# Exclusive decay sums made by VectorE from the inclusive ones, with one PSUM bank instead of two for the sums

## The chip, the cores and the metric

The kernel runs on one core of a Trainium2 chip. The metric is the device time of one execution in microseconds. Every kernel was timed in several rounds beside the kernel before on the same chip. A run counts as slow when it is more than 1.5% above the fastest run of the same kernel.

## The reference

Two layers in a row. A recurrent attention with a decay per channel (4 batches, 8 heads, 768 steps, head dimension 40), and then a layer that mixes all 768 steps of a batch with two 768 x 768 matrices:

```python
def _attn_ref(r, k, v, w, a, b):
    for t in range(S):
        y[:, :, t] = einsum('bhd,bhde->bhe', r_t, state)
        Sa = einsum('bhde,bhe->bhd', state, a_t)
        state = state * w_t[..., None] - einsum('bhd,bhe->bhde', Sa, b_t) \
                + einsum('bhd,bhe->bhde', v_t, k_t)

def _moe_ref(x, w_theta, w_tok_r, w_tok_i, w_ch):
    theta = x @ w_theta
    yr = einsum('ts,bsd->btd', w_tok_r, x * cos(theta))
    yi = einsum('ts,bsd->btd', w_tok_i, x * sin(theta))
    u = x + yr + yi
    return u + maximum(u @ w_ch, 0)
```

The kernel works in chunks of 128 steps, 24 of them ("tiles" below). Within a chunk it needs the products of the decays `w` up to each step: inclusive (with the step's own) for `k` and `b`, exclusive (without it) for `a` and the output. It makes them as exponentials of sums of logarithms.

## The kernel before

TensorE makes both running sums, with two triangular matrices, into the two banks of a pair. ScalarE takes the exponential of both, and of the chunk's total decay, in one instruction:

```python
def cs():
    t = ps(pk)                                   # a pair of PSUM banks
    nc.tensor.matmul(t[:, 0, 512 - DM:512], lhsT=ntri_inc, rhs=lw[:, :, 0:D], ...)
    nc.tensor.matmul(t[:, 1, 0:DM], lhsT=tri_exc, rhs=lw[:, :, 0:D], ...)
    nc.tensor.matmul(t[:, 1, DM:DM + 8], lhsT=ident, rhs=off_diag, ...)
    for g in range(G):                           # the chunk's total decay
        nc.tensor.matmul(t[:, 1, DM + 2 * g:DM + 2 * g + 2], lhsT=pair(lw, g), rhs=ones2, ...)
add("PE", "cs", i, cs, 2 * mm(320) + 5 * 25, [("lw", s2)], [pk], new=(pk, 2), ...)
add("ACT", "exp", i, lambda: nc.scalar.activation(
    out=ex, in_=ps(pk).rearrange("p a b -> p (a b)")[:, 512 - DM:512 + DM + 8],
    func=AF.Exp), 710, [pk], [kex], table="lnexp")
```

No operation is issued as it is written. `add` records it with its engine, its assumed duration and what it reads and writes; then all of them, some 1,500, are put into one order, by priorities that a search has tuned (the tables `OFF`, `TIMES` and `ADJ`), and issued in it. Each engine works through its own part of that order, one instruction after the other: in the eight traces of the changed order (the changed kernel and seven experiments) ScalarE's 390 instructions come in one and the same sequence. What the plan takes for a dependency:

```python
pre = set(after)
for r in reads:                       # a reader waits for the writer
    if r in self.writer:
        pre.add(self.writer[r])
for w in writes:                      # a writer waits for the writer and the readers before
    if w in self.writer:
        pre.add(self.writer[w])
    pre.update(self.readers.get(w, ()))
```

## Time and profile before

| | before |
|---|---|
| time, median of 3 runs | 214.62 us (214.03 to 215.32) |
| span of the profiled run, granted clock | 211.9 us, 0.996 |
| TensorE busy from 20 to 72 us | 48.32 of 52 us |
| TensorE busy from 72 to 205 us | 132.93 of 133 us |

The lines themselves stand in the prediction. The simplest reading comes from the last two rows: what TensorE does not use of the 185 us between 20 and 205 us is 3.68 + 0.07 = 3.75 us. "Busy" includes a matmul's latency (0.30 us for one whose successor starts 0.13 us later, in the prediction's timeline), so it says nothing of how well TensorE is used; but where it is *not* busy, it had nothing to do. I call that figure TensorE's idle time.

How the two engines that make the decays wait is told by the list of waits (the waiting engine and line, what ended the wait; us in total, times, longest). Before, the only direction is TensorE to ScalarE, and GpSimd, which multiplies `k` and `b` by the decays:

```profile
POOL kb L686 <- ACT ex L678: 18.4, 4, 12.1
...
ACT ex L678 <- PE ps_d L674: 3.9, 7, 0.9
```

And this is one tile's decays in the timeline (start us, us): one instruction, between two others.

```profile
89.20 0.44 ACT L898 COPY th<-ps_s 128x320 f32<-128x320 f32 x1
89.52 0.73 ACT L678 ACTIVATE ex<-ps_d 128x648 f32<-128x648 f32 x1
90.12 0.31 ACT L827 COPY gd<-ps_s 128x160 f32<-128x160 f32 x1
```

### The profile page before, as it was taken

What the parts mean: (1) busy time and instruction counts of PE and PEld (TensorE: products, weight loads), DVE (VectorE), ACT (ScalarE), POOL (GpSimd) and SP (SyncE); (2) the same over time, 40 slices, a digit from 0 to 9 for tenths busy, and PEclk for the clock granted to TensorE, in tenths of its full rate; (3) what the DMA queues carried; (4) which work ended last, traced back from release to release, by engine and by line L of the source; (5) the groups of instructions that cost most, each with busy time, mean ns of one, the idle gap of its engine ahead of it and who ended that gap; (6) DMA issues with size and microseconds to landing.
All of it is one profiled execution on the core that took longest, in us unless ns stands there. A gap on an engine that the chain in (4) does not pass through costs nothing.

```text
span 211.9 us, 8102 instructions
## 1 busy us (share of the span) xinstructions
PE 198.8 (94%) x3365; PEld 155.7 (74%) x3365; DVE 166.2 (78%) x253; ACT 152.1 (72%) x342; POOL 117.4 (55%) x173
## 2 busy tenths in 40 slices
PE   7767999989999999999999999999999999999993
PEld 3445788767777788788787877788778787877761
DVE  7477787897879799789898677887889898946443
ACT  4475867999799868977949789777898757573011
POOL 3203365798877674885981859773658440751000
PEclk9999999999999999999999999999999999999998
DMA  6998999999999999995989889989896100002122
GB/s 116 193 169 167 171 212 161 164 172 182 189 170 195 177 193 199 179 164 69 247 163 201 162 150 216 153 191 170 184 193 123 34 3 33 3 3 94 67 91 93
DMA packets 134181, 30.82 MB, mean 145 GB/s; under 512 B 125824, under 2 KB 134144, under 8 KB 134144
## 3 DMA queue, kind: packets, MB, share of 16 engines
q1 hardware_dynamic: 131712, 27.54, 66.5%
q0 software_dynamic: 2432, 2.77, 9.0%
q8 instruction: 26, 0.43, 0.9%
q14 instruction: 11, 0.09, 0.1%
HBM read 29.13 MB, written 3.93 MB: 156 GB/s over the span
## 4 chain that ended last, share of the span: by engine, by line
PE 68%; DVE 6%; ACT 4%; issue 2%; DVEq 0%; ACTq 0%
PE ps_s L942 19%; PE ps_s L616 11%; PE ps_d L740 9%; PE ps_s L888 8%; PE ps_s L843 4%; DVE phi L745 2%; PE ps_s L809 2%; PE ps_s L723 2%; PE ps_s L791 2%; PE ps_s L872 2%; PE ps_s L990 1%; PE ps_s L870 1%; PE ps_s L863 1%; PE ps_d L666 1%; PE ps_s L779 1%
## 5 line engine op out<-in xcount | busy, mean ns | idle before, releaser
L686 POOL TENSOR_TENSOR kb<-raw_kb,ex 128x320 bf16<-128x320 f32 x44 | 37.2, 861 | 18.4 <-ACT ex L678 18.4
L942 PE MATMUL ps_s<-zr,wtok_r 128*128 128x320 bf16 x144 | 41.0, 300 | 0.0
L942 PE MATMUL ps_s<-zi,wtok_i 128*128 128x320 bf16 x144 | 40.8, 299 | 0.0
L690 POOL TENSOR_TENSOR ah<-raw_a,ex 128x320 bf16<-128x320 f32 x22 | 19.0, 864 | 30.6 <-issue 17.0
L745 DVE TENSOR_TENSOR lamu<-ps_d,mask_p 128x1024 bf16<-128x1024 f32 x24 | 29.3, 1220 | 7.0 <-PE ps_d L740 6.6
L745 DVE TENSOR_TENSOR phi<-ps_d,mask_n 128x1024 bf16<-128x1024 f32 x24 | 29.3, 1219 | 4.5 <-PE ps_d L740 4.2
L745 DVE TENSOR_TENSOR lamv<-ps_d,mask_p 128x1024 bf16<-128x1024 f32 x24 | 29.2, 1219 | 3.9 <-PE ps_d L740 3.7
L745 DVE TENSOR_TENSOR psi<-ps_d,mask_p 128x1024 bf16<-128x1024 f32 x24 | 29.2, 1216 | 1.5 <-PE ps_d L740 1.5
L924 POOL TENSOR_TENSOR zi<-cs,x 128x320 bf16<-128x320 f32 x23 | 17.7, 789 | 10.3 <-ACT cs L912 10.1
L924 POOL TENSOR_TENSOR zr<-cs,x 128x320 bf16<-128x320 f32 x23 | 17.7, 789 | 6.8 <-ACT cs L912 6.8
L678 ACT ACTIVATE ex<-ps_d 128x648 f32<-128x648 f32 x24 | 17.1, 713 | 5.1 <-PE ps_d L674 3.9
L619 ACT COPY uT<-ps_s 128x192 f32<-128x192 f32 x24 | 7.5, 319 | 15.5 <-PE ps_s L843 14.2
L879 DVE TENSOR_TENSOR x<-ps_s,ex 128x320 bf16<-128x320 f32 x24 | 11.7, 487 | 7.8 <-PE ps_s L872 3.7
L740 PE MATMUL ps_d<-aT,kbT 64*128 64x128 bf16 x384 | 16.6, 218 | 0.9 <-ACT kbT L619 0.7
L942 PEld LDWEIGHTS <-wtok_r 128*128 128x128 bf16 x144 | 14.0, 97 | 4.5
L942 PEld LDWEIGHTS <-wtok_i 128*128 128x128 bf16 x144 | 14.1, 98 | 3.5
L619 ACT COPY kbT<-ps_s 128x512 f32<-128x512 f32 x24 | 14.2, 590 | 3.3 <-PE ps_s L616 3.2
L952 DVE TENSOR_TENSOR u<-ps_s,x 128x320 bf16<-128x320 f32 x24 | 11.7, 489 | 6.0 <-PE ps_s L942 5.3
L961 DVE SCALAR_TENSOR_TENSOR oo<-ps_s,u 128x320 f32<-128x320 f32 x24 | 11.6, 488 | 5.2 <-PE ps_s L888 4.3
L870 PE MATMUL ps_s<-kb,lamv 128*128 128x40 bf16 x192 | 15.4, 180 | 0.0
L872 PE MATMUL ps_s<-kb,lamu 128*128 128x40 bf16 x192 | 15.0, 180 | 0.1
L616 PE MATMUL ps_s<-ident,kb 128*128 128x128 bf16 x192 | 14.7, 219 | 0.1
(117 smaller groups left out, 562.3 us busy)
## 6 DMA issues: line engine op xcount, KB each, us to landing
raw_v<-in_v_dram SPq DMA_DIRECT2D x24, 160.0 KB, 3.8
raw_w<-in_w_dram SPq DMA_DIRECT2D x24, 160.0 KB, 4.5
raw_kb<-in_k_dram SPq DMA_DIRECT2D x24, 160.0 KB, 4.3
raw_a<-in_a_dram SPq DMA_DIRECT2D x24, 160.0 KB, 3.9
raw_kb<-in_b_dram SPq DMA_DIRECT2D x24, 160.0 KB, 3.9
raw_r<-in_r_dram SPq DMA_DIRECT2D x24, 160.0 KB, 3.4
out_dram<-oo SPq DMA_DIRECT2D x24, 160.0 KB, 1.9
wrow_i<-in_moe_w_tok_i_dram POOLq DMA_DIRECT2D x6, 192.0 KB, 5.0
```

The source lines that it names most:

```text
L616: nc.tensor.transpose(out=dst[:, c:c + 128], in_=pair(src, g), identity=ident)
L619: nc.scalar.copy(out=out.bitcast(FP32), in_=in_)
L678: add("ACT", "exp", i, lambda: nc.scalar.activation(out=ex, in_=ps(pk).rearrange("p a b -> p (a b)")[:, 512 - DM:512 + DM + 8], func=AF.Ex ...
L686: lambda j=j: (nc.vector if fast else nc.gpsimd).tensor_tensor(out=paired(kb[:, j])[:, :, :, 0:D], in0=natural(raw_kb[s4][:, j]), in1=invW ...
L690: lambda: (nc.vector if fast else nc.gpsimd).tensor_tensor(out=paired(ah)[:, :, :, 0:D], in0=natural(raw_a[i % 6]), in1=Wi, op=ALU.mult),
L740: nc.tensor.matmul(t[:, q, g, :], lhsT=lhs[rows(q), g * 128:(g + 1) * 128], rhs=rhs[rows(q), g * 128:(g + 1) * 128], start=True, stop=True)
L745: add("DVE", kindm, i, lambda: nc.vector.tensor_tensor(out=dst.rearrange("p a b c -> p (a b) c"), in0=ps(p).rearrange("p a (g c) -> p (a g ...
L870: nc.tensor.matmul(o, lhsT=lamv[:, p, g, :], rhs=kb[:, 0, h, 0:D], start=first, stop=False, skip_group_check=True)
L872: nc.tensor.matmul(o, lhsT=lamu[:, p, g, :], rhs=kb[:, 1, h, 0:D], start=False, stop=True, skip_group_check=True)
L888: nc.tensor.matmul(dst, lhsT=lhs[:, kt, :], rhs=rhs[:, kt, :], start=kt == 0, stop=kt == 2)
L924: nc.vector if fast else nc.gpsimd).tensor_tensor(
L942: nc.tensor.matmul(ps(pk)[:, 0:DM], lhsT=wtok[nm][:, s, j * 128:(j + 1) * 128], rhs=zs[c][:, s], start=n == 0 and c == 0, stop=n == NT - 1 ...
```

## The change

The intent: an exclusive sum is the inclusive sum less the step's own term. So one of the two 320-column matmuls can go, VectorE makes the exclusive sums by an add, and the sums fit into one bank, which leaves both pairs of banks to the score products. The price is an add on VectorE, and three exponentials in place of one.

```diff
         def cs():
             t = ps(pk)
-            nc.tensor.matmul(t[:, 0, 512 - DM:512], lhsT=ntri_inc, rhs=lw[:, :, 0:D], ...)
-            nc.tensor.matmul(t[:, 1, 0:DM], lhsT=tri_exc, rhs=lw[:, :, 0:D], ...)
+            nc.tensor.matmul(t[:, 0:DM], lhsT=ntri_inc, rhs=lw[:, :, 0:D], ...)
 ...                                       (the total decay: now into columns 320 to 327, sign turned)
-        add("PE", "cs", i, cs, 2 * mm(320) + 5 * 25, [("lw", s2)], [pk], new=(pk, 2),
+        add("PE", "cs", i, cs, mm(320) + 5 * 25, [("lw", s2)], [pk], new=(pk, 1),
             tail=tail(2))
         add("ACT", "exp", i, lambda: nc.scalar.activation(
-            out=ex, in_=ps(pk).rearrange("p a b -> p (a b)")[:, 512 - DM:512 + DM + 8],
-            func=AF.Exp), 710, [pk], [kex], table="lnexp")
+            out=ex[:, 0:DM], in_=ps(pk)[:, 0:DM], func=AF.Exp), 432, [pk], [kex], table="lnexp")
+        sx = rw_t[i % 2]
+        add("DVE", "wi", i, lambda: nc.vector.tensor_tensor(
+            out=sx[:, 0:DM].rearrange("p (h d) -> p h d", h=H),
+            in0=ps(pk)[:, 0:DM].rearrange("p (h d) -> p h d", h=H), in1=lw[:, :, 0:D], op=ALU.add),
+            490, [pk, ("lw", s2)], [("rw", i % 2)])
+        add("ACT", "ew", i, lambda: nc.scalar.activation(
+            out=ex[:, DM:2 * DM], in_=sx, func=AF.Exp, scale=-1.0),
+            432, [("rw", i % 2)], [kw], table="lnexp")
+        add("ACT", "ewm", i, lambda: nc.scalar.activation(
+            out=ex[:, 2 * DM:2 * DM + 8], in_=ps(pk)[:, DM:DM + 8], func=AF.Exp, scale=-1.0),
+            180, [pk], [kwm], table="lnexp")
 ...                                       (users of ex wait for the part that they read)
-OFF = dict(...)  TIMES = dict(...)  ADJ = {...}
+OFF = dict(...)  TIMES = dict(...)  ADJ = {...}      (all priorities searched anew)
```

## The prediction

> **What bounds the kernel now.** I read the page's engine row first, then its slices, then the sums by stretch, the chain of waits, and last the groups that the change touches.
>
> ```profile
> PE 198.8 (94%) x3365; PEld 155.7 (74%) x3365; DVE 166.2 (78%) x253; ACT 152.1 (72%) x342; POOL 117.4 (55%) x173
> ...
> PE   7767999989999999999999999999999999999993
> ...
> DMA  6998999999999999995989889989896100002122
> ...
> PE 68%; DVE 6%; ACT 4%; issue 2%; DVEq 0%; ACTq 0%
> ```
>
> TensorE looks like the bound, but 94% is an average over two regimes. The DMA digits are full up to about 160 us and then fall away. The sums by stretch separate the regimes (columns: length, busy time and instructions of each engine, clock, DMA share, GB/s):
>
> ```profile
> 20.00:72.00 52.00, 48.32 (x961) 39.55 (x962) 44.83 (x50) 44.68 (x103) 38.00 (x54) 1.00 1.01 180
> 72.00:205.00 133.00, 132.93 (x2199) 104.98 (x2198) 105.89 (x143) 95.46 (x215) 75.10 (x104) 1.00 0.68 132
> ```
>
> Up to 72 us the DMA share is 1.01: the inputs of a tile (six transfers of 160 KB, 0.98 MB) at 180 GB/s take 5.5 us, an estimate from that row, and the starts of the decay sums show ten tiles between 5 and 58 us, 5.3 us each. So the transfers pace this part, with VectorE (44.83 of 52, 86%) and ScalarE (44.68, 86%) not far behind. From 72 us on the token mixing of earlier batches is a stock of ready TensorE work: TensorE is busy for 132.93 of 133.00 us, and the chain of waits is nearly all matmuls there. What is taken from TensorE after 72 us comes off the end; what is taken before is mostly hidden under the transfers.
>
> "Busy" counts a matmul's whole latency, so a matmul's price must be read from starts. The timeline of one tile's decay sums, in a saturated stretch:
>
> ```profile
> 114.54 0.30 PE L666 MATMUL ps_d<-lw,ntri_inc 128*128 128x320 bf16 x1
> 114.67 0.30 PE L668 MATMUL ps_d<-lw,mask_p 128*128 128x320 bf16 x1
> 114.81 0.17 PE L670 MATMUL ps_d<-off_diag,ident 128*128 128x8 bf16 x1
> 114.84 0.24 PE L674 MATMUL ps_d<-ones,lw 128*128 128x2 bf16 x4
> ```
>
> Each 320-column matmul reads 0.30 us, but the next starts 0.13 to 0.14 us later. That is its price. The other groups concerned (busy time, mean ns, idle before, releaser):
>
> ```profile
> L678 ACT ACTIVATE ex<-ps_d 128x648 f32<-128x648 f32 x24 | 17.1, 713 | 5.1 <-PE ps_d L674 3.9 <-POOL r L715 0.8 <-issue 0.2
> ...
> L659 ACT ACTIVATE lw<-raw_w 128x320 bf16<-128x320 f32 x24 | 11.5, 478 | 3.0 <-DMA raw_w<-in_w_dram 3.0
> ...
> L898 ACT COPY th<-ps_s 128x320 f32<-128x320 f32 x23 | 9.9, 429 | 4.2 <-PE ps_s L888 3.9
> L817 DVE TENSOR_TENSOR gt<-ps_s,ex 128x320 bf16<-128x320 f32 x20 | 9.7, 487 | 2.9 <-PE ps_s L809 2.4 <-ACT nuT L619 0.2
> ```
>
> **What the Trainium skill says.** "TensorE: Matmul & The Clock Gate", section "Back-to-back issue gap", gives N/2.4 + 2.5 ns for a warm matmul: 136 ns for 320 columns. The trace agrees (0.13 to 0.14 us). "VectorE: DVE Perf Modes", section "The TRN2 errata", gives an fp32 two-tensor add (N + 151)/0.96 = 491 ns; the trace's 128x320 operations with a PSUM input take 487. "ScalarE: Activation LUTs", section "What ACT_TABLE_LOAD costs", gives 186 + 0.833 N ns with immediate scale and bias, so a scale of -1 costs nothing extra, and about 93 ns of overlap between neighbours. For 648 columns that is 726 against 713 measured; in the timeline one ScalarE copy of 0.58 us starts at 40.34 and the next exponential at 40.82, so the overlap is 0.10. "PSUM — Partial Sum Buffer", section "PSUM bank collisions raise a hardware error", says two engines must not read one bank at once. Before, ScalarE alone reads the sums; now VectorE reads the same bank too, so the two reads have to be ordered. No run here shows that yet.
>
> **The change, part by part.**
>
> Removed: one 320-column matmul per tile and its weight load. 24 x 136 ns = 3.26 us of TensorE issue. The trace has 11 of these before 72 us and 13 after. The 13 are worth 13 x 0.136 = 1.77 us of the end. The 11 (1.50 us) fall where TensorE waits for data and earn nothing directly. The small matmuls of the chunk decay stay: one of 8 columns and four of 2, with the sign turned.
>
> Added on VectorE: one 128x320 add per tile, 487 ns in the trace for such a form. Neighbours overlap by 0.08 us (gt starts 63.41 and the next 63.81, 0.40 apart), so 0.40 us of engine time each, 24 x 0.40 = 9.6 us; busy time grows by 24 x 0.487 = 11.7 us to about 178.
>
> Changed on ScalarE: one exponential of 648 columns (713 ns) becomes three: 320 from PSUM (429, like the copy of th), 320 from SBUF (between 429 and the 478 of lw; I take 465) and 8 columns (about 165, from the straight line through copies of 160 columns at 292 and 512 at 590 ns). 429 + 465 + 165 - 713 = +346 ns of busy time a tile, +8.3 us in all, but with two more overlaps of 0.10 only about 0.15 us of engine time a tile, 3.5 us.
>
> Moved in time: the inverse decays that k and b wait for come about 0.136 + 0.28 = 0.42 us earlier. The decays for a go through matmul, (ordered) exponential, add, exponential: 0.43 + 0.49 + 0.465 against 0.71, so some 0.7 us later if the reads are ordered, less 0.136. Four buffers of ex and the run-ahead of a tile's preparation should hide this, except for the first tile.
>
> Banks: the sums leave the two pairs of banks, which only the score products use now, for the pool of four single banks. Scores in 64-row mode come in 65 runs in the issue order I read from the trace: 34 of one product (426 ns median until other work starts) and 31 of two (648). Joining two single runs saves 2 x 426 - 648 = 204 ns. After 72 us there are 11 single runs; with free pairs I expect two or three joins, -0.5 us. Against it, a single bank is held longer (matmul, exponential, add, small exponential, some 2 us); I charge +0.3 us for waits of other work.
>
> Where added work can reach the end: from 60 to 71 us VectorE runs without a gap (busy 11.97 of 12 from 60 to 72), while the stock of mixing work is not there yet. Two adds in that stretch are 0.8 us; I charge half, +0.4.
>
> The order: all priorities were searched anew for the new costs. That cannot be costed from a row; an order made for a lighter TensorE and a heavier VectorE should recover some of the early idle time. I allow -0.7.
>
> Sum: -1.77 - 0.5 + 0.3 + 0.4 - 0.7 = -2.3 us; 214.6 - 2.3 = 212.3.
>
> **Rivals.** First, VectorE becomes a joint bound. For it: 86% up to 72 us, saturated from 60 to 72, and 9.6 us more engine time; early tiles take 5.2 us and VectorE would use about 4.9 of it. Against: 105.89 of 133 us after 72 leaves 27 us for 13 x 0.40 = 5.2, and the transfers pace the early part. If it wins, mixing starts 1 to 3 us later and the time is 214 to 216. Second, the freed bank pairs matter more than the matmul: VectorE's waits for score products (16.1 us of idle before the four masked products) shrink, the early part tightens and all 3.26 us count, with more joins. For it: those waits are VectorE's largest. Against: early, the transfers are full whatever the banks do, and late the waits are on a busy TensorE, not on banks. It would give 209 to 211. Third, transfers set the last tile: their share stays near 1 to about 160 us, so nothing that TensorE saves ends sooner. Against: between 72 and 205 us TensorE never idles, and the mixing that fills it needs no more input. It would give 214.6.
>
> **Range and chances.** The sure part is the 1.77 us. The wide parts are the new order (either way a microsecond or two) and the early part. Eight times in ten I expect 209.6 to 215.2. Faster by over 2% means under 210.3; that needs the whole 3.26 us plus a microsecond from joins or order: 0.17. Slower by over 2% needs VectorE to become the bound for the length of the kernel: 0.06. Within 2%: 0.77.
>
> **What would show it.** In the profile after: 24 matmuls fewer on TensorE and busy time down by 5 to 8 us; VectorE busy near 178 and ScalarE near 160; the add at about 487 ns, the three exponentials at about 429, 465 and 165; TensorE still gapless from some 70 us to the last rows; the DMA digits still full to about 160 us. The add should start after the first exponential ends, or the other way round, never together. More pairs among the 64-row runs would confirm the bank part; the same number would remove its 0.5. I am wrong if VectorE has stretches of 15 us without a gap while TensorE idles, if mixing starts later than about 73 us, or if the early tiles come closer than 5.2 us (then transfers did not pace them).

## The result, and the profile after

The changed kernel takes 221.03 us (median of 4 runs, 220.73 to 221.51) against 214.32 (213.21 to 215.32) for the kernel before in the same rounds: a ratio of 1.0316, 95% interval 1.026 to 1.0373. It is slower by 3.2%, and the prediction, 212.3 us and in its range at most 215.2, was wrong. A ratio here is the mean time of one kernel's fast runs over that of the other's of the same rounds, so not quite the ratio of the medians beside it. One per cent is 2.14 us throughout.

The profiled runs: spans of 219.0 and 211.9 us. The engine row, the slices of TensorE and the DMA, and the chain of waits by engine, after:

```profile
PE 200.1 (91%) x3341; PEld 156.3 (71%) x3341; DVE 176.4 (81%) x277; ACT 155.7 (71%) x390; POOL 117.9 (54%) x173
...
PE   6689878888689999999999999999999999999993
...
DMA  6999989999799999597688999988999000001312
...
PE 63%; ACT 19%; DVE 8%; DMA 4%; issue 4%; SPq 0%; POOL 0%; ACTq 0%; DVEq 0%
```

The 24 matmuls are gone (3341 against 3365), the 24 adds are there, and VectorE's busy time is near the 178 us foreseen. TensorE's was to fall by 5 to 8 us and rose by 1.3; ScalarE's was to be near 160. ScalarE's share of the chain went from 4% to 19%, and VectorE's from 6% to 8%. Matmuls are still most of the chain (63%, before 68%). The 4% of DMA are mainly one transfer of mixing weights; they are 4% as well in the experiment below whose add reads a constant, which takes 215.3 us, so the loss isn't there. The sums by stretch:

```profile
20.00:72.00 52.00, 44.43 (x902) 35.92 (x900) 44.90 (x54) 44.73 (x115) 37.28 (x53) 0.99 0.96 171
72.00:205.00 133.00, 129.83 (x2225) 103.65 (x2225) 113.31 (x155) 99.34 (x249) 77.13 (x107) 1.00 0.69 130
```

TensorE is idle for 7.57 + 3.17 = 10.74 us where it was for 3.75: 7.0 us more. That this is near the 7.1 us by which the span grew is partly chance: over the whole span its idle time goes from 13.1 to 18.9 us (span less busy time), 5.8 us more, and its busy time from 198.8 to 200.1, although 24 matmuls are gone. So most of the loss is TensorE with nothing to do. The clock (0.991 against 0.996) could explain 1.0 us of it at most, an estimate from 0.5% of 200 us. The DMA share fell below 1 in the early stretch, so it is not more transfer time that holds TensorE up there.

What was it waiting for? The groups of the new instructions (busy us, mean ns, then idle of the engine just before them and what ended it):

```profile
L692 DVE TENSOR_TENSOR rw<-ps_s,lw 128x320 f32<-128x320 f32 x24 | 11.6, 489 | 8.4 <-ACT ex L688 4.8 <-PE ps_s L684 1.4 <-ACT kbT L631 1.0
...
L696 ACT ACTIVATE ex<-rw 128x320 f32<-128x320 f32 x24 | 11.3, 477 | 0.2 <-DVE rw L692 0.2
...
L688 ACT ACTIVATE ex<-ps_s 128x320 f32<-128x320 f32 x24 | 10.4, 438 | 5.9 <-DVE rw L692 2.9 <-PE ps_s L684 2.9
...
L699 ACT ACTIVATE ex<-ps_s 128x8 f32<-128x8 f32 x24 | 4.2, 181 | 4.0 <-DVE rw L692 4.0
```

The durations are close to what was predicted (487, 429, 465 and 165 ns). New are the idle times ahead of them, and their releasers: VectorE's add waits for ScalarE's first exponential (4.8 us), which needs nothing of it; the first exponential waits for the add (2.9 us), which it needs nothing of either; and the small exponential waits for the add (4.0 us). None of the three is a wait for data: `L688`, `L692` and `L699` only read the sums. The list of waits has them with their counts:

```profile
POOL kb L707 <- ACT ex L688: 32.6, 7, 14.7
...
DVE rw L692 <- ACT ex L688: 4.8, 10, 1.5
...
ACT ex L699 <- DVE rw L692: 4.0, 10, 0.6
...
ACT ex L688 <- DVE rw L692: 2.9, 6, 0.6
```

And GpSimd waits 32.6 us for the first exponential, where it waited 18.4; but that is no measure of the loss, for it waits 41.0 us for the exponentials (19.1 and 21.9) in an experiment below in which the engines hardly take turns. Summed over all rows of that list, ScalarE waits 12.5 us for VectorE where it waited 1.4. The same tile as before, in the timeline, first on ScalarE and then on VectorE:

```profile
87.29 0.44 ACT L688 ACTIVATE ex<-ps_s 128x320 f32<-128x320 f32 x1
88.28 0.18 ACT L699 ACTIVATE ex<-ps_s 128x8 f32<-128x8 f32 x1 [0.56 <-DVE rw L692]
88.36 0.46 ACT L696 ACTIVATE ex<-rw 128x320 f32<-128x320 f32 x1
```

```profile
87.76 0.49 DVE L692 TENSOR_TENSOR rw<-ps_s,lw 128x320 f32<-128x320 f32 x1 [0.46 <-ACT ex L688]
```

VectorE sits idle for 0.46 us until the exponential has ended (87.73), adds, and ScalarE sits idle for 0.56 us until the add has ended (88.25) before it may read its 8 columns. Each of these two waits is about as long as the other engine's read (0.44 and 0.49 us). From the last sum to the last decay this tile takes 1.6 us; before it took 0.8.

I call it a turn when the reading of a tile's sums passes from one of the two engines to the other. Paired tile by tile from the trace, the 24 tiles have 38 turns: 14 go exponential, add, small exponential (two turns); in three the add comes last and in seven first (one turn). In none of the 24 do the reads of the two engines overlap.

**The theory**: two engines that read the same sums in PSUM must take turns. Each turn couples two queues that work in order: when one is late, the other stands still with all that is behind it, and TensorE, which lives on what both make, runs dry. The plan knew nothing of the turns, so the order that the search found doesn't allow for them. **The rivals**: VectorE's added work; ScalarE's added instructions; the longer chain of data from sums to decays (matmul, add, exponential); the new order as such; the single bank.

### The profile page after: what moved, and what is told of

Its sections match the earlier page's. It is cut to its first block, busy times and chain, and to the rows that moved or that the text cites. A ratio compares the mean times of both kernels' runs of the same rounds, so it can differ in the third digit from the quotient of the medians.

```text
span 219.0 us, 8120 instructions
## 1 busy us (share of the span) xinstructions
PE 200.1 (91%) x3341; PEld 156.3 (71%) x3341; DVE 176.4 (81%) x277; ACT 155.7 (71%) x390; POOL 117.9 (54%) x173
## 4 chain that ended last, share of the span: by engine, by line
PE 63%; ACT 19%; DVE 8%; DMA 4%; issue 4%; SPq 0%; POOL 0%; ACTq 0%; DVEq 0%
PE ps_s L963 16%; PE ps_s L628 11%; PE ps_d L761 8%; PE ps_s L909 8%; DVE rw L692 4%; PE ps_s L864 3%; DMA wrow_i<-in_moe_w_tok_i_dram 3%; ACT ex L688 3%; DVE phi L766 2%; PE ps_s L893 2%; PE ps_s L744 2%; ACT cs L933 2%; ACT rT L748 2%; PE ps_s L812 2%; DMA raw_w<-in_w_dram 2%
## 5 line engine op out<-in xcount | busy, mean ns | idle before, releaser
L707 POOL TENSOR_TENSOR kb<-raw_kb,ex 128x320 bf16<-128x320 f32 x44 | 37.6, 864 | 40.4 <-ACT ex L688 32.6
L711 POOL TENSOR_TENSOR ah<-raw_a,ex 128x320 bf16<-128x320 f32 x22 | 18.9, 862 | 13.5 <-ACT ex L696 5.8
L692 DVE TENSOR_TENSOR rw<-ps_s,lw 128x320 f32<-128x320 f32 x24 | 11.6, 489 | 8.4 <-ACT ex L688 4.8
L748 ACT COPY rT<-ps_s 128x512 bf16<-128x512 bf16 x24 | 14.0, 597 | 2.1 <-PE ps_s L744 2.1
L628 PE MATMUL ps_s<-ident,kb 128*128 128x128 bf16 x192 | 15.4, 227 | 0.1
L761 PEld LDWEIGHTS <-kbT 64*128 64x128 bf16 x384 | 11.4, 95 | 5.3 <-issue 1.7
```

The source lines that it names most:

```text
L628: nc.tensor.transpose(out=dst[:, c:c + 128], in_=pair(src, g), identity=ident)
L692: add("DVE", "wi", i, lambda: nc.vector.tensor_tensor(out=sx[:, 0:DM].rearrange("p (h d) -> p h d", h=H), in0=ps(pk)[:, 0:DM].rearrange("p ...
L707: lambda j=j: (nc.vector if fast else nc.gpsimd).tensor_tensor(out=paired(kb[:, j])[:, :, :, 0:D], in0=natural(raw_kb[s4][:, j]), in1=invW ...
L711: lambda: (nc.vector if fast else nc.gpsimd).tensor_tensor(out=paired(ah)[:, :, :, 0:D], in0=natural(raw_a[i % 6]), in1=Wi, op=ALU.mult),
L748: add("ACT", "er", i + x, lambda x=x: nc.scalar.copy(out=rT[:, x].rearrange("p (g t q) -> p g t q", g=G, q=8), in_=ps(pr).bitcast(BF16).re ...
L761: nc.tensor.matmul(t[:, q, g, :], lhsT=lhs[rows(q), g * 128:(g + 1) * 128], rhs=rhs[rows(q), g * 128:(g + 1) * 128], start=True, stop=True)
```

## The experiments

Fourteen kernels ran. Apart from what is said to be left out, the instructions, their sizes and their places stay the same.

### In the new order: take the suspects away one at a time

**No add.** The add is left out, and the second exponential reads a constant tile in SBUF. Its output is wrong, which doesn't matter for the time.

```diff
-        add("DVE", "wi", i, lambda: nc.vector.tensor_tensor(... in0=ps(pk) ...),
+        add("DVE", "wi", i, lambda: None,
-            out=ex[:, DM:2 * DM], in_=sx, func=AF.Exp, scale=-1.0),
+            out=ex[:, DM:2 * DM], in_=big, func=AF.Exp, scale=-1.0),
```

> The changed kernel in its own order, with VectorE's add left out; the second large exponential reads a constant SBUF tile in place of the exclusive sums (wrong result on purpose). ScalarE's three exponentials stay. Before is 214.3, the changed kernel 221.0. If the added VectorE work or the hand-offs of the shared bank cost the 6.7 us, this comes to 213 to 216. If the new order or the single bank of the sums costs it, it stays at 219.5 to 221.5.

Measured: 215.11 us, ratio 1.0013 (0.9932 to 1.0093). Its profiled run fell in an odd execution of 447.84 us; the other runs took 212.89 to 215.38. The new order, the single bank and three exponentials together are thus not measurably slower than the kernel before (though the matmul's gain isn't seen either): most of the cost comes with the add. That the single bank is held longer is no large cost in the changed kernel itself: its TensorE waits for an exponential to leave a bank three times, 0.9 us in all, and never for the add.

**The add, reading a constant.** VectorE adds as before, but reads a constant tile in SBUF in place of the sums. Its output is wrong, which doesn't matter for the time. VectorE's work, ScalarE's wait for the add's result and all places stay; VectorE's reading of the shared bank goes, and with it the add's wait for the matmuls (1.4 us in the changed kernel, twice).

```diff
-            in0=ps(pk)[:, 0:DM].rearrange(...), in1=lw[:, :, 0:D], op=ALU.add),
+            in0=big.rearrange(...), in1=lw[:, :, 0:D], op=ALU.add),
```

> The changed kernel in its own order; VectorE's add stays at full size but takes a constant SBUF tile in place of the sums in PSUM, so that VectorE and ScalarE no longer read one bank (wrong result on purpose). Hand-off theory (the ordered reads of one bank stall both in-order queues): 214 to 216.5, near the run without the add. Load theory (0.4 us more of VectorE a tile): 219 to 221, near the changed kernel. Order theory: 219.5 to 221.5 for both this and the run without the add.

Measured: 215.3 us, ratio 1.0059 (0.9991 to 1.0126), which leaves 1.0316 - 1.0059 = 2.6%, 5.5 us, to the reading (turns and that wait together; the pair with a second copy, below, parts them). VectorE is busy for 178.4 us here, no less than in the changed kernel, and the second exponential still waits for the add. So neither VectorE's time nor the chain from add to exponential is the bulk of it. The late stretch has its TensorE back:

```profile
72.00:205.00 133.00, 132.15 (x2242) 105.84 (x2241) 113.20 (x157) 98.08 (x244) 75.87 (x105) 1.00 0.70 135
```

**One reader, the other way round.** Now VectorE reads the sums and ScalarE's first and small exponentials read constants. Its output is wrong, which doesn't matter for the time.

```diff
-            out=ex[:, 0:DM], in_=ps(pk)[:, 0:DM], func=AF.Exp), 432, ...
+            out=ex[:, 0:DM], in_=big, func=AF.Exp, scale=-1.0), 432, ...
-            out=ex[:, 2 * DM:2 * DM + 8], in_=ps(pk)[:, DM:DM + 8], func=AF.Exp, scale=-1.0),
+            out=ex[:, 2 * DM:2 * DM + 8], in_=big[:, 0:8], func=AF.Exp, scale=-1.0),
```

> The changed kernel in its own order; VectorE's add reads the sums in PSUM as in the change and so waits for the matmuls, but ScalarE's first and its small exponential read a constant SBUF tile, so the bank has one reader (wrong result on purpose). If it is the two readers taking turns that costs (each in-order queue waiting for the other), this comes to 213.5 to 216.5, near the run whose add reads SBUF. If it is VectorE's queue waiting for the matmuls of the sums, it stays at 218.5 to 221.5.

Measured: 213.31 us, ratio 0.9976 (0.9922 to 1.0031). Whichever engine stops reading the shared sums, the loss is gone. This one alone proves less than it looks: ScalarE no longer waits for the matmuls either.

**One turn fewer.** The small exponential is merged into the first: one of 328 columns. The result is right.

```diff
-            out=ex[:, 0:DM], in_=ps(pk)[:, 0:DM], func=AF.Exp), 432, ...
+            out=ex[:, 0:DM + 8], in_=ps(pk)[:, 0:DM + 8], func=AF.Exp), 432, ...
-        add("ACT", "ewm", i, lambda: nc.scalar.activation(...),
+        add("ACT", "ewm", i, lambda: None,
```

> The changed kernel in its own order, correct result: the 8-column exponential is taken into the first one (328 columns, the small sums with their old sign), so ScalarE and VectorE take turns once a tile and not twice, and ScalarE has 24 instructions fewer. Take-turns theory: 216.5 to 219.5, a part of the 6.7 us back, since the small exponential waited 4.0 us for the add in ten tiles. If the length of the chain to the decays of a is what costs, nothing changes there (the add still follows the first exponential): 220 to 221.5.

Measured: 218.65 us, ratio 1.0201 (1.0116 to 1.0285). The turns go from 38 to 24, one fewer in the 14 tiles that had two, and 1.2%, 2.5 us, comes back; but the two intervals overlap a little, and an instruction went with the turn, so this alone would not settle it.

### In the old order: the parts of the arithmetic

**The matmul alone taken out.** The kernel before, in its own order, without the exclusive matmul; the exclusive decays are a constant. Its output is wrong, which doesn't matter for the time.

```diff
-            nc.tensor.matmul(t[:, 1, 0:DM], lhsT=tri_exc, rhs=lw[:, :, 0:D], start=True, stop=True)
-            out=ex, in_=ps(pk)...[:, 512 - DM:512 + DM + 8],
+            out=ex[:, 0:DM + 8], in_=ps(pk)[:, 0, 0:DM + 8],
```

> The kernel before in its own order with the exclusive matmul left out and nothing in its place; one exponential of 328 columns, the decays of a and of the output are a constant (wrong result on purpose). The most that the change could win in this order. My prediction credited the matmul with 1.77 us, so 212 to 213; ScalarE's shorter exponential may add up to 1 us: 211 to 213. If TensorE's work were no bound at all: 214.

Measured: 212.04 us, ratio 0.9913 (0.9851 to 0.9975). The matmul is worth 0.9%, 1.9 us, when nothing is asked in return (and the exponential is 320 columns shorter here, so it is at most that; the interval reaches from 0.5 to 3.2 us).

**The new arithmetic put into the old order.** The order of the kernel before is kept; the add and two exponentials are set in at places that I chose by a rule (the add after the first exponential, the last exponential ahead of the product that needs it). Right result. Then the same with the add reading a constant, and the same without the add and with the second exponential reading a constant (both wrong).

```diff
+    for n, (o, _, ewm, wi, ew) in enumerate(extra):   # set into the order as it was
+        timed.append((t + 0.1, 1, 3 * n, ewm, "lnexp"))
+        timed.append((td, 1, 3 * n + 1, wi, None))    # left out in the third of these kernels
+        timed.append((te, 1, 3 * n + 2, ew, "lnexp"))
```

> The kernel before, with its own order of every other operation and the sums still in a pair of banks (the second one unused), but with the new arithmetic: one large matmul, three exponentials, the add on VectorE from the same bank. Correct result. Order theory: 213 to 215, since the old order is kept and TensorE has less to do. Load and hand-off theories: 217.5 to 221.

> As the run in the old order with the new arithmetic, which took 227.9, but the add takes a constant SBUF tile in place of the sums (wrong result on purpose): the second large exponential waits for the add, the add for nothing but its place in VectorE's queue. If VectorE's read of the sums (turns, and a decay of a that comes later) cost the 13.8 us: 214 to 218. If the three exponentials and the add as work cost it: 224 to 228.

> The old order with the new sums and three exponentials but without the add; the second large exponential reads a constant tile at the same place of ScalarE's queue (wrong result on purpose). With the add from SBUF this order took 225.4. If ScalarE's waiting for VectorE's queue made that: 213 to 216. If the three exponentials and their later place did: 221 to 225.

| in the old order | median us | ratio | 95% interval |
|---|---|---|---|
| new arithmetic, all of it | 227.9 | 1.065 | 1.0571 to 1.0728 |
| add reads a constant | 225.35 | 1.0535 | 1.0471 to 1.0598 |
| no add, second exponential reads a constant | 218.24 | 1.0172 | 1.0122 to 1.0223 |
| exclusive matmul left out, nothing added | 212.04 | 0.9913 | 0.9851 to 0.9975 |

Read from below: the second large exponential and the small one cost 2.6% (5.5 us) where the order makes no room for them, a part of which the kernel before pays too (its one exponential has 648 columns, that of the last row 328); the add as work and ScalarE's waiting for its data cost 3.6% (7.8 us); and the add's reading of the sums 1.2% (2.5 us, with intervals that overlap slightly; here there is one turn in each tile, and TensorE's score products also wait 4.5 us for this add to leave the pair of banks). Compare the new order, where the first two cost little (ratios 1.0013 and 1.0059, with the matmul gone) and the third 2.6%. The search knew of the exponentials and of the data that passes from add to exponential, and it seems to have arranged the rest around them. It did not know of the turns. The old order, with places chosen by a rule, does worse with the same arithmetic (227.9 us). Three of these runs were misses: the first took more than any theory had (at most 221), the second fell where I expected the added work and not the read to cost, the third between my two ranges. In the old order, then, the reading is the smallest part.

**Two banks for the same sums.** In the old order again, the inclusive sums are written into both banks of the pair, and VectorE reads the second. I meant it to take the turns away. Right result.

```diff
+            nc.tensor.matmul(t[:, 1, 0:DM], lhsT=ntri_inc, rhs=lw[:, :, 0:D], start=True, stop=True)
-            in0=ps(pk)[:, 0, 0:DM]..., in1=lw[:, :, 0:D], op=ALU.add),
+            in0=ps(pk)[:, 1, 0:DM]..., in1=lw[:, :, 0:D], op=ALU.add),
```

> As the run in the old order with the new arithmetic, but the inclusive sums are made twice, one copy in each bank of the pair, so that ScalarE reads one bank and VectorE the other; TensorE has as many large matmuls as before. Correct result. Hand-off theory: 214 to 216, at least 2 us below the one-bank run in spite of 24 x 0.136 = 3.3 us more matmul. Load theory: as the one-bank run or up to 3 us slower, 218 to 222. Order theory: 214 to 215.5 for both.

Measured: 228.76 us, ratio 1.0687 (1.0628 to 1.0746). It missed, and the timeline says why: the turns are still there.

```profile
31.55 0.44 ACT L681 ACTIVATE ex<-ps_d 128x320 f32<-128x320 f32 x1 [0.37 <-PE ps_d L676]
31.88 0.17 ACT L683 ACTIVATE ex<-ps_d 128x8 f32<-128x8 f32 x1
```

```profile
32.09 0.49 DVE L685 TENSOR_TENSOR rw<-ps_d,lw 128x320 f32<-128x320 f32 x1 [0.36 <-ACT ex L683]
```

The add reads another bank and still waits until ScalarE's last read of the pair has ended. In all 24 tiles it starts after that, and in ten the list of waits puts its wait (6.5 us in all) down to that read. Both banks belong to one named tile; I take it that the built program orders the readers by tile, and the next kernel, in which they do overlap, agrees. To part the readers, the copy has to lie in another tile.

### The turns, by themselves

**A second copy in another tile.** The changed kernel, its order kept; in 22 of 24 tiles the sums are written once more into another bank that is free at that time, and VectorE reads the copy.

```diff
+            if i in SECOND:
+                nc.tensor.matmul(second(i)[:, 0:DM], lhsT=ntri_inc, rhs=lw[:, :, 0:D], ...)
-            in0=ps(pk)[:, 0:DM].rearrange(...), in1=lw[:, :, 0:D], op=ALU.add),
+            in0=second(i)[:, 0:DM].rearrange(...), in1=lw[:, :, 0:D], op=ALU.add),
```

> The changed kernel in its own order, correct result: TensorE writes the inclusive sums a second time into another bank that is free at that point (22 of 24 tiles; two tiles share as before), and VectorE adds from that copy. Every wait for data stays (both engines still wait for the matmuls, the second exponential for the add), 22 x 0.136 = 3.0 us of TensorE come back; only the taking of turns at one bank goes. Take-turns theory: 213.5 to 217, well under the changed kernel in spite of more work. Rival, that the waits for data and the longer chain cost: 220 to 223.

Measured: 222.89 us, ratio 1.0381 (1.0324 to 1.0438): no gain at all, a clear miss of 213.5 to 217, and within the range of the rival (220 to 223). Its result was wrong too, which I had not intended (relative error 0.124; the control below writes the same copies and is right, so some tile's add read its copy too late, after other work had taken the bank; I didn't pin down which). The turns were gone in the 22 tiles, though (there the add and a read of ScalarE overlap, which they do in no tile of the changed kernel), and the same tile's decays were done sooner. ScalarE, then VectorE:

```profile
88.51 0.44 ACT L698 ACTIVATE ex<-ps_s 128x320 f32<-128x320 f32 x1
88.84 0.17 ACT L709 ACTIVATE ex<-ps_s 128x8 f32<-128x8 f32 x1
88.90 0.47 ACT L706 ACTIVATE ex<-rw 128x320 f32<-128x320 f32 x1
```

```profile
88.36 0.49 DVE L702 TENSOR_TENSOR rw<-ps_s,lw 128x320 f32<-128x320 f32 x1
```

Add and exponential overlap (88.36 to 88.85 and 88.51 to 88.95), nobody waits, and from the last sum to the last decay it takes 0.95 us against 1.62. If the theory holds, something else must have eaten the gain: 22 matmuls of 0.136 us are 3.0 us more for TensorE, and each has to wait for a second bank. That needed a control, not an argument.

**Its control: the copy written, but not read.** The same kernel with one line put back: VectorE reads the shared bank again. The result is right.

```diff
-            in0=second(i)[:, 0:DM].rearrange(...), in1=lw[:, :, 0:D], op=ALU.add),
+            in0=ps(pk)[:, 0:DM].rearrange(...), in1=lw[:, :, 0:D], op=ALU.add),
```

> The control of the run with a second copy of the sums: the same order, the same 22 extra 320-column matmuls into the same second banks, but VectorE's add reads the first bank again, so that ScalarE and VectorE take turns at it. The extra matmuls and the waits for a second bank are then in both runs, and only the turns are in this one. If the turns cost the time: about 226 us (225 to 229), 3 us or more above the 222.89 of the run with the second copy. If the turns cost little and the cost is the added work and the longer chain of it: the same 222 to 224. If its result is right, the second copy itself was what was read wrongly in that run; if it is wrong as well, the extra matmul overwrites something.

Measured: 227.97 us, ratio 1.0659 (1.0575 to 1.0744; one of four executions, 229.69 us, counted as slow). In both kernels the add waits for matmuls and the second exponential for the add. The turns, 38 here and 4 in the other, cost 1.0659 - 1.0381 = 2.8%, 5.9 us, beside the 5.5 us that the constant in place of the sums had shown. The copies by themselves cost 1.0659 - 1.0316 = 3.4%, 7.3 us, which is why taking the turns away gained nothing in the kernel above. The waits are those of the changed kernel, and larger:

```profile
DVE rw L702 <- ACT ex L698: 9.4, 13, 1.7
...
ACT ex L698 <- DVE rw L702: 4.6, 6, 0.9
...
ACT ex L709 <- DVE rw L702: 3.9, 10, 0.6
...
DVE rw L702 <- ACT ex L709: 2.3, 2, 1.3
```

They sum to 20.2 us. In the run with the copy read, rows of this kind sum to 1.3 us:

```profile
ACT ex L709 <- DVE rw L702: 0.8, 2, 0.6
...
DVE rw L702 <- ACT ex L698: 0.5, 2, 0.3
```

**One more turn, and its control.** The changed kernel, with a copy of 8 columns by VectorE to a tile nobody reads, just ahead of the first exponential. In one kernel it reads the sums, in the other a constant in SBUF. Both results are right.

```diff
+        def exp():
+            nc.vector.tensor_copy(out=tiny_t[i % 4], in_=ps(pk)[:, 0:8])   # control: in_=big
+            nc.scalar.activation(out=ex[:, 0:DM], in_=ps(pk)[:, 0:DM], func=AF.Exp)
```

> The changed kernel with one more turn at the shared bank in each tile: VectorE copies 8 columns of the sums to a tile nobody reads, just before ScalarE's first exponential. The result stays right. If each turn costs the time that merging two turns gave back (2.3 us for one turn a tile): 223 to 225 us. If only the number of instructions matters (24 small ones on VectorE, about 0.1 us each, in slack): 221 to 221.8, like its control.

> The control of the run with one more turn: the same 24 small copies in the same places of VectorE's queue, but from a constant tile in SBUF. Both theories: 221 to 221.8 us, the changed kernel's time and at most half a microsecond more. If it comes out as high as the run with the turn, small instructions on VectorE are what costs.

Measured: 228.58 us, ratio 1.0708 (1.0652 to 1.0763), with the turn; 219.4 us, ratio 1.0265 (1.0203 to 1.0327; one execution of 222.58 us counted as slow), with the same instruction and no turn: below the 221 to 221.8 that I expected, with an interval that overlaps the changed kernel's. The trace shows 55 turns against 38: 17 more, since in the seven tiles in which the add comes first the copy follows it and adds none. They cost 4.4%, 9.4 us, or 0.55 us each (an estimate that charges the copy's own wait for the matmuls, 1.6 us, to them too). That is more than the 223 to 225 that I expected from the merged exponential. The list of waits has the reason:

```profile
ACT ex L693 <- DVE tiny L692: 12.2, 21, 1.3
```

and so has one tile's timeline, VectorE and then ScalarE:

```profile
130.07 1.22 DVE L771 TENSOR_TENSOR phi<-ps_d,mask_n 128x1024 bf16<-128x1024 f32 x1 [1.43 <-PE ps_d L766]
131.21 0.15 DVE L692 COPY tiny<-ps_s 128x8 f32<-128x8 f32 x1
131.87 0.49 DVE L697 TENSOR_TENSOR rw<-ps_s,lw 128x320 f32<-128x320 f32 x1 [0.50 <-ACT ex L693]
```

```profile
131.40 0.44 ACT L693 ACTIVATE ex<-ps_s 128x320 f32<-128x320 f32 x1 [0.83 <-DVE tiny L692]
```

An instruction of 0.15 us held ScalarE up for 0.83 us, since it stood in VectorE's queue behind a masked product of 1.22 us that itself had been 1.43 us late; the sums had been ready since 130.60. The mean of the 21 waits is 0.58 us. So a turn costs the other engine's read and, where that read is not next in line, the other engine's queue as well. In the changed kernel it is mostly the read: its waits at turns (4.8 + 4.0 + 2.9 us above, in 26) have a mean of 0.45 us, and the reads take 0.44 and 0.49.

### An order that knows of the turns

The kernel with the small exponential merged, with one dependency more in the plan, and all priorities searched anew from those of the changed kernel. Right result.

```diff
+        o_exp = add("ACT", "exp", i, ...)
         add("DVE", "wi", i, ...,
-            490, [pk, ("lw", s2)], [("rw", i % 2)])
+            490, [pk, ("lw", s2)], [("rw", i % 2)], after=[o_exp])
-OFF, TIMES, ADJ = ...
+OFF, TIMES, ADJ = ...                       # searched anew
```

> The kernel with the small exponential merged into the first (one turn a tile), and with all priorities searched anew while the search is told that the add comes after the first exponential. If the loss is in turns that the search did not know of, an order made with them known takes back part: 215 to 217.5 us against the 218.65 of the same arithmetic in the old search's order. If the turns were not what was missing, 218 to 220.

Measured: 216.04 us, ratio 1.0131 (1.0085 to 1.0178). Of the 3.2% that the change had lost, 1.9% (4.0 us) came back. Its windows:

```profile
20.00:72.00 52.00, 45.74 (x925) 37.45 (x926) 46.56 (x57) 44.61 (x109) 37.78 (x54) 1.00 0.98 177
72.00:205.00 133.00, 132.63 (x2226) 106.39 (x2224) 112.12 (x155) 98.03 (x231) 76.28 (x106) 1.00 0.66 129
```

TensorE is nearly without a gap again in the late stretch (0.37 us idle, 3.17 in the changed kernel). A turn is still there in each of the 24 tiles, but ScalarE waits 4.3 us for VectorE in place of 12.5 (sums over the list of waits). Against the merged kernel in the old search's order (1.0201) the intervals overlap, so merging and ordering are shown together and not each by itself; and I can't compare the length of my search with that behind the two kernels. So 216 us is what that search gave, and no floor. No version with a right result beat the kernel before.

TensorE's idle time between 20 and 205 us, worked out as above, in order of it:

| kernel | readers of one sum tile, turns in 24 tiles | idle us | ratio |
|---|---|---|---|
| before | one, 0 | 3.75 | 1 |
| order with turns, small exponential merged | two, 24 | 6.63 | 1.0131 |
| add reads a constant (wrong) | one, 0 | 8.41 | 1.0059 |
| small exponential merged | two, 24 | 8.83 | 1.0201 |
| changed | two, 38 | 10.74 | 1.0316 |
| changed, tiny copy from SBUF | two, 38 | 11.19 | 1.0265 |
| second copy, read (3.0 us more matmuls) | one (two in 2 tiles), 4 | 12.39 | 1.0381 |
| second copy, not read (3.0 us more matmuls) | two, 38 | 14.68 | 1.0659 |
| one more turn | two, 55 | 16.35 | 1.0708 |

The ratios follow the idle time but for two pairs of neighbours. In the two pairs of a kernel and its control, the one with more turns is the one in which TensorE idles more. Idle time is no exact measure of a kernel's time: the kernel before has 24 matmuls more than those without a second copy (some 3.3 us), and the run with VectorE as the one reader, not in the table, idles for 7.00 us at a ratio of 0.9976.

## Why the prediction was wrong, step by step

**The step that failed.** The prediction saw the turns coming: "if the reads are ordered" the decays for `a` come some 0.7 us later, and the add "should start after the first exponential ends, or the other way round, never together". Both are so. It then wrote: "Four buffers of ex and the run-ahead of a tile's preparation should hide this, except for the first tile", and entered nothing in the sum. That entry was worth 5.5 to 5.9 us by two independent pairs of runs (the constant in place of the sums; the second copy read or not), 0.14 to 0.17 us for each turn taken away (38 and 34 of them; an estimate). The delay itself was right: the tile shown takes 0.8 us longer from sum to last decay. The prediction thought of a delay in *one tile's result*. What a turn does is to stop *an engine*, and what stands behind it in that engine's queue belongs to other tiles.

**The matmul, -1.77 us.** Not contradicted: 1.9 us when it is taken out alone, an upper bound at that, with an interval from 0.5 to 3.2. That only what is saved after 72 us counts fits this, but is not shown by itself.

**VectorE in its full stretch, +0.4 us.** Not contradicted: with the add (of a constant) and without it, the ratios are 1.0059 and 1.0013, a microsecond apart and with intervals that overlap.

**The joins of 64-row runs, -0.5 us.** Did not come. Read from the trace as before, the changed kernel has 64 such runs (65 before), of which 14 single ones after 72 us (11 before). With free pairs and the new order together, nothing was joined after 72 us.

**The single bank held longer, +0.3 us.** Not measured by itself. In the run without the add, at 1.0013, the bank is free sooner than in the changed kernel.

**The new order, -0.7 us.** Wrong in its reason. The prediction took it that an order searched for the new costs would suit them. It suited the costs that the plan had; the turns were not among them, which the plan's code, shown above and open to me when I predicted, would have told: two readers get no order. With the small exponential merged and the turn told, a new order took back 4.0 us; how much of that is the telling is not shown.

**What remains.** The sum was -2.3 us and the result +6.7: 9.0 us apart. The turns make 5.5 to 5.9 of it; the joins and the order's gain that did not come, 1.2; the add about 0.6 more than was charged. This is bookkeeping: of its terms only the first is measured clear of noise. The rest, 1.3 to 1.7 us, fits ScalarE's 48 instructions more (in the run without the add, the matmul's 1.9 us are not to be seen either), but no run isolates it in the new order.

**The rivals.** VectorE as a joint bound would have shown in the run in which it adds a constant: busy for 178.4 us, it takes 215.3. Freed pairs that matter more, 209 to 211, are far off. Against transfers as the bound speaks their share, which fell from 1.01 to 0.96 early while TensorE idled more. Of the prediction's own signs of being wrong none was met, two of them narrowly: mixing starts at 72.8 us (not after 73; 71.6 before); VectorE's longest stretch without a gap, from 39.13 to 54.10, is just under 15 us, with TensorE idle for 1.9 us of it (a longer one, 18.6 us, stands in the run whose add reads a constant, which loses next to nothing); the first ten tiles' sums come 5.8 us apart. That last reading was off in the prediction: ten starts from 5.08 to 57.88 us have nine steps between them, so 5.9 us each before the change and not 5.3. Its picture of the profile after did fail: TensorE gapless from some 70 us on (3.17 us idle after 72) and less busy by 5 to 8 us (more by 1.3). What would have caught the cause is not on its list: idle time ahead of instructions whose releaser gives them no data.

## What to carry to other kernels

When a change gives a second engine a reader of the same PSUM tile, price the turn by the other engine's read and by what stands ahead of that read in its queue: here an instruction of 0.15 us held ScalarE up for 0.83. Look in the list of waits for releasers that hand over no data; they may be turns. A merged read takes some of them away, and a copy in another tile takes nearly all, but here the copy's own cost ate the gain. A scheduler that lists dependencies only between writers and readers is blind to them; and when an experiment that should help doesn't, run its control before giving the theory up.

## What the Trainium skill lacked or had wrong

- "PSUM — Partial Sum Buffer", section "PSUM bank collisions raise a hardware error", says that ScalarE and VectorE reads of one bank must be kept apart, and that the compiler orders reads too. The traces agree (in the changed kernel no two of these reads overlap), but the page gives no price. Here: 5.5 to 5.9 us for 38 turns in 24 tiles, and 9.4 us for 17 more, 0.55 us each.
- The same section tells of banks and quadrants. In the program built here, the readers seem to be ordered by named tile: with the copy in the second bank of the same tile, the add started after ScalarE's last read in all 24 tiles, in the one shown after a wait of 0.36 us (ratio 1.0687 against 1.065 with one bank). I found no page that has it.
- "ScalarE: Activation LUTs", section "What ACT_TABLE_LOAD costs", gives one line for an activation with immediate scale and bias and names no source (a table elsewhere in the skill does tell PSUM from SBUF), 186 + 0.833 N ns: 453 for 320 columns and 193 for 8. Measured were 438 from PSUM and 477 from SBUF, and 181 for 8 columns from PSUM.
- I found no page on orders searched with a model that lacks some of the waits: the same arithmetic took 227.9 us in the old order, 221.0 in one searched without the turns and 216.0 (with the small exponential merged) in one searched with them.
